# Decode attention plus bilinear GLU on one core: the query weights of head 0 leave the first load and come with the second

## The chip, the cores and the metric

The kernel runs on one core of a Trainium2 chip. The metric is the device time of one execution in microseconds (us). The kernel before the change takes 377.63 us, the median of three runs (377.3 to 377.72). One more execution was taken with the hardware profiler: it took 377.5 us, and the trace of it spans 375.7 us; some 1.8 us of the time lie around the span.

## The reference

One token is decoded for a batch of two, in float32. `x` has 2 rows of 512 values. It is normalised to `xn` (mean and variance over the 512), and three things are added:

```python
xn = _layernorm(x, axis=-1)
return x + _A_ref(xn, A_k_cache, A_v_cache, A_wq, A_wo) + _B_ref(xn, B_w_gate, B_w_up, B_w_down)
# A: q = xn @ wq (32 heads of 128); scores = q . K / sqrt(128); p = softmax(scores); o = p . V; o @ wo
#    K and V: the last 2048 positions of each head's cache, for each of the two batch rows
# B: ((xn @ w_gate) * (xn @ w_up)) @ w_down, inner width 1376
```

Nearly all data are the caches: 2 x 32 x 2048 x 128 values for K and as many for V, each used once.

## The kernel before, in words

**The stream.** All inputs but a small copy of `x` are laid out on the host in one DRAM array, `stream`, in the order in which they are used. `blocks()` (L43 to L79) lists the loads: each is a list of fields (kind, index, width in floats for each of the 128 partitions). Each load is one DMA of 128 rows, one row to a partition. The first load goes to a tile of its own, `first`, that stays; the others go to three rotating buffers, `step`, of 13,824 floats a partition (`BUFS = 3`). `pump()` (L141) issues loads on SP's queue, in order, until all three buffers are taken. `done()` (L164) counts the fields of a buffer; when the last field is used the buffer is free, and `pump()` issues the next load into it.

In the kernel before, the loads begin so (rows in floats for each partition; 4 bytes each):

| load | fields | floats in a row | KB in all |
|---|---|---|---|
| first | x (8), columns of ones: pick, rows, carry (31), w of head 0 (512) | 551 | 275.5 |
| step 0 | w of heads 1 to 3 (1536), K and wq of heads 0 and 1 | 10752 | 5376 |
| step 1 | half of w_gate and w_up, K and wq of head 2 | 12800 | 6400 |
| step 2 | the other half, K3, V0, K4 and their weights, parts of w_down | 13440 | 6720 |
| step 3 on | three K or V units each | 13824 | 6912 |

Here `wq` beside K of head h is a quarter of the query weights of the group of four heads after h's own. The query weights of heads 0 to 3 alone are needed at once; they are the fields `w 0` (head 0) and `w 1` (heads 1 to 3).

**The start.** DVE (VectorE) and PE (TensorE) make the layer norm from `x` (L211 to L229) and spread `xn` over 128 columns each (`xnb`), so that a matmul with it puts q into all 128 partitions. `project_first(0)` then multiplies `xnb` with `w 0` into a part of the PSUM tile `tr` (8 matmuls of 128 columns, which the trace shows as 16 passes), and `project_first(1)` multiplies it with `w 1` into the PSUM tile `q` (8 matmuls of 384 columns, 16 passes). Both stand in the code in this order, in a loop ahead of the heads, and each engine runs its instructions in the order of the code (the class `InOrder`).

**A head.** For head h: `products(h)` on DVE multiplies K by q in place (4096 elements a partition), `project_q(h)` on PE makes a part of a later group's q, `sums(h)` on DVE adds over the 128 elements and frees K, `maxima(h)` finds the largest score, `weights(h)` makes the exponentials on ACT (ScalarE); POOL (GpSimd) reduces over partitions. `products(0)` reads q from `tr`; `products(1)` to `products(3)` read it from the tile of `project_first(1)`. Three heads later `values` multiplies with V on PE and adds the output projection into `acc`. `project_gu` and `gate` (heads 2 and 3) do the GLU between. The last loads are small pieces, so that little is left to do when the last one lands.

In the trace almost every instruction has line L97, that of the helper in `InOrder`, so groups are told apart by engine, tile and shape.

Of the kernel before, what the change touches and what calls it, by code (L numbers as in the profile page):

```python
# [17 lines left out]
B, D, H, DH, SK, F = 2, 512, 32, 128, 8192, 1376  # L18
W = min(4096, max(256, SK // 4))
J = W // P  # L20
NC = D // P
# [12 lines left out]
CK, CQ, CO = B * J * DH, NC * GC, D  # L34
# [9 lines left out]
def blocks():  # L44

    def wd(n):
        return [("wd", i, D) for i in range(*WD[n])]

    def k(h):
        return [("k", h, CK)] + ([("wq", h, CP)] if h + HG < H else [])

    def v(h):
        return [("v", h, CK), ("wo", h, CO)]  # L60

    def gu(half):
        n = NC * (FH[half][1] - FH[half][0])
        return [("wg", half, n), ("wu", half, n)]

    units = []
    for h in range(LAG, H - 1):
        units += [k(h), v(h - LAG)]
    ones = [("pick", 0, 8 * B), ("rows", 0, NFB * B), ("carry", 0, M)]
    first = [("x", 0, B * NC)] + ones + [("w", 0, NC * DH)]  # L70
    loads = [[("w", 1, CQ - NC * DH)] + k(0) + k(1), gu(0) + k(2)]
    loads += [gu(1) + units[0] + units[1] + wd(0) + [("wr", 0, NS * P)]]
    loads += [sum(units[i : i + 3], []) for i in range(2, len(units), 3)]
    loads += [k(H - 1) + v(H - 1 - LAG) + wd(1)]
    out = [(("f", 0), first)] + [(("s", i), fields) for i, fields in enumerate(loads)]
    late, last = ("s", len(loads)), ("s", len(loads) + 1)
    out += [(late, v(H - 3)), (late, v(H - 2)), (last, [("v0", H - 1, CL)])]
    out += [(last, [("v1", H - 1, CK - CL)]), (last, [("wo", H - 1, CO)] + wd(2))]
    return out + [(last, wd(n)) for n in range(3, len(WD))]  # L79
# [33 lines left out]
def kernel(  # L113
# [19 lines left out]
    for key, fields in blocks():  # L133
        todo.append((key, fields, at))
        at += P * sum(w for _, _, w in fields)
# [312 lines left out]
    for _, fields in blocks():  # L448
        ks = [i for kind, i, _ in fields if kind == "k"]
        vs = [i for kind, i, _ in fields if kind == "v"]  # L450
        if vs and vs[-1] >= H - 5:
            break
        for n, h in enumerate(ks):
            products(h)
            project_q(h)
            if 2 <= h <= 3:
                project_gu(h - 2)
            sums(h)
            if h == LAG:
                gate()  # L460
            if vs and n == 0:
                values(vs)
            if h == LAG:
                down(0)
                down_rest()
            maxima(h)
            weights(h)
            if h >= 1:
                reciprocals(h - 1)
# [52 lines left out]
def laid_out(x):  # L522
# [3 lines left out]
    a = x["A_x"].reshape(B, D)  # L526
    first = {
        kind: np.zeros((P, w), a.dtype) for kind, _, w in blocks()[0][1][:4]
    }
    first["x"][:] = a.reshape(B, P, NC).transpose(1, 0, 2).reshape(P, B * NC)  # L530
# [83 lines left out]
```

## Time and profile before

| | |
|---|---|
| time, median of 3 runs | 377.63 us (377.3 to 377.72) |
| profiled execution | 377.5 us, its span 375.7 us |
| PE busy | 254.2 us in 1084 matmul passes |
| DVE busy | 294.1 us in 146 instructions |
| ACT busy | 58.6 us |
| POOL busy | 25.3 us |
| bytes moved by DMA | 159.70 MB, 425 GB/s over the span |

Times in the trace are microseconds from the start of the span. A row of the timeline has start, duration, engine, line, operation, the tile written and the tiles read, the shape, the count, and in brackets how long the engine had been idle before and what ended it. A row of the table by stretch has, for each engine, the busy time in the stretch and the number of instructions, then the granted clock of PE (1.00 is full), the share of the time in which the 16 DMA engines were busy (short stretches can show more than 1, since a packet is put down to where it starts) and the rate. A line of DMA issues has the size of one and the time from its issue to its landing.

### The profile page before, as it was taken

The numbers are of one execution on the slowest core, as the hardware profiler recorded it, in microseconds if no ns is written. First come the engines' busy times: TensorE is split into PE (matmuls) and PEld (weight loads), VectorE is DVE, ScalarE is ACT, GpSimd is POOL, SyncE is SP. The second block draws the span as 40 slices with busy tenths as digits, with TensorE's granted clock in tenths as the row PEclk, the third lists the DMA queues.
The fourth block names the chain that finished last, engine by engine and source line by source line (L and its number), as shares of the span: only waits on it lengthen the run. The fifth ranks groups of instructions, "written<-read, shape, count | busy, mean of one in ns | idle before, by whom it ended". The sixth has DMA issues, their size and how long they took to land.

```text
span 375.7 us, 2858 instructions
## 1 busy us (share of the span) xinstructions
PE 254.2 (68%) x1084; PEld 88.5 (24%) x1084; DVE 294.1 (78%) x146; ACT 58.6 (16%) x259; POOL 25.3 (7%) x78
## 2 busy tenths in 40 slices
PE   3496497886547486854858476685846669637996
PEld 3241023331112122211212121231212122212334
DVE  3299691998599499769949976994996799599950
ACT  1021001122021111201112020211202011211131
POOL 1001000000000000100000100000000000000010
PEclk9998967998697666888768696885869676857999
DMA  8999999899999999999999999999999999999995
GB/s 346 445 436 454 426 408 471 383 465 449 395 466 406 442 455 400 459 418 436 460 400 449 424 430 459 402 442 430 430 459 406 437 444 436 419 431 443 398 421 221
DMA packets 4492, 159.70 MB, mean 425 GB/s; under 512 B 512, under 2 KB 640, under 8 KB 1152
## 3 DMA queue, kind: packets, MB, share of 16 engines
q1 hardware_dynamic: 4480, 159.54, 98.5%
q8 instruction: 8, 0.13, 0.1%
q14 instruction: 4, 0.03, 0.0%
HBM read 159.48 MB, written 0.06 MB: 425 GB/s over the span
## 4 chain that ended last, share of the span: by engine, by line
DMA 63%; DVE 26%; PE 8%; ACT 1%; issue 0%; SPq 0%; DVEq 0%
DMA step<-in_stream_dram 63%; DVE s L97 13%; DVE step L97 13%; PE o_ps L97 3%; PE q L97 2%; PE acc L97 2%; PE tr L97 1%; ACT o_sb L97 0%; DVE m L97 0%; ACT oT L97 0%; SPq L97 0%; DVE rec L97 0%; DVE o_out L97 0%; DVEq L97 0%
## 5 line engine op out<-in xcount | busy, mean ns | idle before, releaser
L97 DVE TENSOR_TENSOR step<-step,q 128x4096 f32<-128x4096 f32 x31 | 136.6, 4407 | 52.4 <-DMA step<-in_stream_dram 52.4
L97 PE MATMUL q<-step,xnb 128*128 128x512 f32 (+1 forms) x128 | 92.4, 872 | 76.4 <-DMA step<-in_stream_dram 76.4
L97 DVE TENSOR_REDUCE s<-step 128x32 f32<-128x4096 f32 x32 | 141.4, 4419 | 1.1
L97 PE MATMUL o_ps<-step,p 128*16 128x512 f32 x512 | 68.9, 672 | 11.5 <-DMA step<-in_stream_dram 11.5
L97 PEld LDWEIGHTS q<-step,xnb 128*128 128x128 f32 x128 | 32.3, 275 | 130.5 <-DMA step<-in_stream_dram 77.5
L97 PE MATMUL acc<-step,oT 128*9 128x512 f32 (+1 forms) x88 | 35.4, 552 | 9.3 <-ACT oT L97 8.1
L97 PE MATMUL tr<-first,o_sb 128*128 128x2 f32 (+2 forms) x198 | 28.1, 261 | 15.4 <-ACT o_sb L97 13.0
L97 ACT COPY o_sb<-o_ps 128x512 f32<-128x512 f32 (+1 forms) x25 | 14.1, 568 | 140.7 <-PE o_ps L97 140.7
L97 PEld LDWEIGHTS tr<-first,o_sb 128*128 128x128 f32 x198 | 26.0, 200 | 36.8 <-ACT o_sb L97 32.4
L290 POOL PARTITION_ALL_REDUCE mm<-m x32 | 11.3, 354 | 283.1 <-DVE rec L97 180.1
L97 PEld LDWEIGHTS o_ps<-step,p 128*16 128x16 f32 x512 | 13.4, 104 | 69.9 <-issue 54.4
L97 ACT ACTIVATE nm<-mm 128x2 f32<-128x2 f32 x32 | 6.5, 203 | 131.4 <-POOL mm L290 131.4
L97 ACT ACTIVATE p<-s,nm 128x16 f32<-128x16 f32 x64 | 19.2, 300 | 1.0
L97 ACT ACTIVATE oT<-tr,rec 128x1 f32<-128x1 f32 x64 | 12.2, 260 | 28.5 <-PE tr L97 28.5
L306 POOL PARTITION_ALL_REDUCE sum<-rs x32 | 12.7, 398 | 55.0 <-ACT p L97 55.0
L97 PE MATMUL o_ps<-step,xn 128*2 128x512 f32 (+1 forms) x48 | 13.9, 616 | 0.0
L97 ACT ACTIVATION_READ_ACCUMULATOR p<-s,nm 128x1 f32 x64 | 12.0, 187 | 0.0
L97 DVE TENSOR_TENSOR step<-step,tr 128x4096 f32<-128x4096 f32 x1 | 4.4, 4422 | 9.3 <-DMA step<-in_stream_dram 9.3
L97 PEld LDWEIGHTS acc<-step,oT 128*9 128x9 f32 x88 | 4.5, 91 | 19.4 <-ACT oT L97 12.7
L97 PE MATMUL q<-xnb,mean_w 128*128 128x512 f32 (+2 forms) x18 | 8.3, 551 | 0.0
L97 DVE TENSOR_TENSOR o_out<-acc,x_nat 128x128 f32<-128x128 f32 x1 | 0.3, 292 | 8.8 <-PE acc L97 8.8
L97 DVE TENSOR_REDUCE m<-s 128x2 f32<-128x32 f32 x32 | 5.9, 186 | 1.1
(39 smaller groups left out, 40.5 us busy)
## 6 DMA issues: line engine op xcount, KB each, us to landing
step<-in_stream_dram SPq DMA_DIRECT2D x16, 6912.0 KB, 31.1
step<-in_stream_dram SPq DMA_DIRECT2D x2, 6400.0 KB, 32.8
step<-in_stream_dram SPq DMA_DIRECT2D x1, 6720.0 KB, 45.4
step<-in_stream_dram SPq DMA_DIRECT2D x1, 6656.0 KB, 29.0
step<-in_stream_dram SPq DMA_DIRECT2D x1, 5376.0 KB, 15.3
step<-in_stream_dram SPq DMA_DIRECT2D x1, 4864.0 KB, 29.6
step<-in_stream_dram SPq DMA_DIRECT2D x2, 2304.0 KB, 17.1
step<-in_stream_dram SPq DMA_DIRECT2D x1, 1536.0 KB, 14.6
```

The source lines that it names most:

```text
L97: made = call(*args, **kwargs)
L290: nc.gpsimd.partition_all_reduce(mm, m, P, bass_isa.ReduceOp.max)
L306: nc.gpsimd.partition_all_reduce(sum_t[h], rs, P, bass_isa.ReduceOp.add)
```

## The change

The first load keeps only `x` and the columns of ones: 39 floats, 156 bytes a row. `w 0` moves to the front of step 0, whose rows grow from 10752 to 11264 floats. Nothing else is changed: `project_first(0)` finds its weights in the step buffer, and its `done("w", 0)` now counts towards freeing that buffer. The order of the instructions on every engine is as before, and so is the number of DMAs.

```diff
     ones = [("pick", 0, 8 * B), ("rows", 0, NFB * B), ("carry", 0, M)]
-    first = [("x", 0, B * NC)] + ones + [("w", 0, NC * DH)]
-    loads = [[("w", 1, CQ - NC * DH)] + k(0) + k(1), gu(0) + k(2)]
+    first = [("x", 0, B * NC)] + ones
+    w = [("w", 0, NC * DH), ("w", 1, CQ - NC * DH)]
+    loads = [w + k(0) + k(1), gu(0) + k(2)]
     loads += [gu(1) + units[0] + units[1] + wd(0) + [("wr", 0, NS * P)]]
```

## The prediction

> **What bounds the kernel now.** I read the page first, then a table by stretch, then the timeline of the first 70 us and of the end.
>
> ```profile
> PE 254.2 (68%) x1084; PEld 88.5 (24%) x1084; DVE 294.1 (78%) x146; ACT 58.6 (16%) x259; POOL 25.3 (7%) x78
> ...
> DMA  8999999899999999999999999999999999999995
> ...
> q1 hardware_dynamic: 4480, 159.54, 98.5%
> q8 instruction: 8, 0.13, 0.1%
> ...
> DMA 63%; DVE 26%; PE 8%; ACT 1%; issue 0%; SPq 0%; DVEq 0%
> ```
>
> DVE is busy for 78% of the span and PE for 68%, but the 16 DMA engines for 98.5%: their line is 8 or 9 in every slice until the last. The chain of waits puts 63% on the arrival of `step` loads. Its 26% on DVE are no bound of their own: that chain goes from a load's issue back to the DVE work that freed the buffer, and whether the issue was late has to be looked at by itself. The table by stretch shows that it was not (columns: the five engines' busy time, PE's granted clock, share of DMA, GB/s):
>
> ```profile
> 3.50:16.40 12.90, 4.93 (x20) 4.49 (x20) 1.83 (x9) 0.26 (x1) 0.00 (x0) 1.00 1.01 437
> 16.40:47.40 31.00, 22.44 (x60) 8.02 (x60) 27.03 (x11) 3.97 (x16) 2.26 (x6) 0.93 1.01 436
> 47.40:65.10 17.70, 15.23 (x46) 5.79 (x50) 9.70 (x5) 1.71 (x8) 0.35 (x1) 0.69 0.96 413
> 65.10:81.40 16.30, 13.70 (x64) 4.88 (x56) 16.05 (x6) 3.56 (x16) 1.15 (x3) 0.94 1.00 434
> 81.40:340.70 259.30, 166.80 (x650) 52.50 (x648) 216.08 (x97) 39.86 (x184) 18.06 (x48) 0.76 1.00 433
> ```
>
> From 3.5 us to 340.7 us the share is 1.00 or 1.01 and the rate 433 to 437 GB/s in every stretch but one: in 47.4 to 65.1 us a load takes 17.7 us where the next takes 16.3. So the loads flow one behind the other with no hole, and each load's place in time is the sum of the bytes ahead of it. The end hangs on them too:
>
> ```profile
> 372.49 0.12 PEld L97 LDWEIGHTS acc<-step,hT 128*9 128x9 f32 x8 [0.30 <-DMA step<-in_stream_dram]
> 372.96 0.29 DVE L97 TENSOR_TENSOR o_out<-acc,x_nat 128x128 f32<-128x128 f32 x1 [8.80 <-PE acc L97]
> ```
>
> The weight load of PE's last group waited 0.30 us for the last load's landing; 0.47 us later DVE makes the last addition. The time is therefore: when the stream begins, plus 159.5 MB at its rate, plus a tail of some 3.2 us from 372.49 to 375.7.
>
> **The change part by part: the stream.** No byte is added. 512 floats a row (256 KB over 128 rows) go from the first load to the second. Both are in front of everything else, so all later loads start after the same bytes, 551 + 10752 = 39 + 11264 floats a row. What can differ is the start.
>
> SP's rows of the timeline to 40 us, one line on the packets that began by 1.73 us, and the issues to 2.8 us (size, time to landing):
>
> ```profile
> 0.72 0.38 SPq L97 DMA_DIRECT2D first<-in_stream_dram  x1
> 1.16 1.37 SPq L97 DMA_DIRECT2D step<-in_stream_dram  x3
> 2.57 0.54 SPq L97 DMA_DIRECT2D x_nat<-in_x_rows_dram  x1
> 34.54 0.33 SPq L97 DMA_DIRECT2D step<-in_stream_dram  x1
> ```
>
> ```profile
> DMA packets 2, 0.00 MB, mean 3 GB/s; under 512 B 0, under 2 KB 0, under 8 KB 2
> ```
>
> ```profile
> step<-in_stream_dram SPq DMA_DIRECT2D x1, 6720.0 KB, 45.4
> step<-in_stream_dram SPq DMA_DIRECT2D x1, 6400.0 KB, 30.0
> step<-in_stream_dram SPq DMA_DIRECT2D x1, 5376.0 KB, 15.3
> first<-in_stream_dram SPq DMA_DIRECT2D x1, 275.5 KB, 2.9
> ```
>
> SP issues the first load at 0.72 and the next three from 1.16 in a row of 1.37 us, some 0.46 each. Two packets had begun by 1.73, so data starts to flow 1.0 us after its issue. First (275.5 KB) takes 2.9 us to landing; the load after it (5376 KB) lands 15.3 us after its issue, thus at 16.5. Now the first transfer shrinks to 19.5 KB. What its eight rows for each engine cost is bounded by a transfer of rows of a like size, the output at the end (56 KB in rows of 512 bytes; its stretch is 373.0 to 375.7):
>
> ```profile
> q1 hardware_dynamic: 128, 0.06, 7.6%
> ```
>
> 7.6% of 2.7 us are 0.205 us an engine for 8 packets, 26 ns each. For 156 bytes I take at most that, 0.2 us. The 256 KB that move cost 0.60 us at 437 GB/s, in the first load or in the second. So two ends. If the second load's data flow as soon as the small rows are through, the stream keeps its place, or gains at most some 0.1 us, the price of eight separate packets an engine. If the second load cannot flow sooner than it does now (its issue at 1.16 is not moved; today the share of DMA is full from 3.5 on, as the first load lands), the 0.60 us are in full a hole: +0.6 us. By the issue, 0.44 us after the first one and with the same 1.0 us to first data, it can flow from 2.2 us, about when the small rows end. That is near the lower end: I take **+0.1 us**. Nothing hides it: this cost is on the path in full.
>
> [...]
>
> **The change part by part: q of head 0 comes late.** PE's and DVE's rows of the timeline:
>
> ```profile
> 7.20 3.75 PE L97 MATMUL tr<-first,xnb 128*128 128x128 f32 x16 [1.53 <-issue]
> 16.52 11.84 PE L97 MATMUL q<-step,xnb 128*128 128x384 f32 x24 [5.57 <-DMA step<-in_stream_dram]
> 31.62 2.65 PE L97 MATMUL q<-step,xnb 128*128 128x512 f32 x4 [3.26 <-DMA step<-in_stream_dram]
> 34.20 8.02 PE L97 MATMUL o_ps<-step,xn 128*2 128x512 f32 x32
> ```
>
> ```profile
> 16.58 4.42 DVE L97 TENSOR_TENSOR step<-step,tr 128x4096 f32<-128x4096 f32 x1 [9.33 <-DMA step<-in_stream_dram]
> ...
> 25.59 4.41 DVE L97 TENSOR_TENSOR step<-step,q 128x4096 f32<-128x4096 f32 x1
> ...
> 47.48 4.42 DVE L97 TENSOR_TENSOR step<-step,q 128x4096 f32<-128x4096 f32 x1 [3.67 <-DMA step<-in_stream_dram]
> ...
> 65.25 4.42 DVE L97 TENSOR_TENSOR step<-step,q 128x4096 f32<-128x4096 f32 x1 [7.16 <-DMA step<-in_stream_dram]
> ```
>
> The 16 passes into `tr` ran from 7.20 to 10.95, while the second load was under way; DVE then waited 9.33 us for that load alone. Now they too wait for it. PE starts at 16.52 as before, but with these 16 passes: 3.75 us, from 16.5 to 20.3. The row is taken as it is: those passes followed an idle PE (1.53 us, and small passes before), and so will these, after a longer one. `products(0)` follows the last pass instead of the landing (PE's 16.52 and DVE's 16.58 stand side by side today), so **DVE starts 3.75 us later**, at 20.3. The moved wait holds up, on PE, the 16 passes of heads 1 to 3 and `project_q`; on DVE, the two memsets are ahead of it and everything else behind.
>
> PE's groups by shape to 31 us:
>
> ```profile
> L97 PE MATMUL q<-step,xnb 128*128 128x384 f32 x16 | 8.4, 703 | 5.6 <-DMA step<-in_stream_dram 5.6
> L97 PE MATMUL tr<-first,xnb 128*128 128x128 f32 x16 | 3.8, 429 | 1.5 <-issue 1.5
> L97 PE MATMUL q<-step,xnb 128*128 128x512 f32 x8 | 3.6, 592 | 0.0
> ```
>
> On PE, the 16 passes of heads 1 to 3 (8.4 us) then end at 28.7 instead of 24.9. `products(1)` wants them when DVE is there: 25.59 + 3.75 = 29.3, so 0.6 us to spare. They cannot take longer than in the trace, where they followed 5.6 us of idle PE; even 1 us more would only add itself to DVE's delay. Behind them the 8 passes of `project_q` (3.6 us) end at 32.3, 0.7 us after the 31.62 at which PE now waits for the next load; `project_gu` (34.20, 8.02 us) then ends at 42.9 at the latest, before DVE has done head 2.
>
> Who waits for DVE? First, SP: the fourth `step` load is issued at 34.54, when head 1's sums free the first buffer. It becomes 38.3. Its data are wanted when the third load is through; that landed 45.4 us after its issue at about 2.1, thus at 47.5. With 1.0 us from issue to data it has to be issued by 46.5: 12 us to spare today, **8.2 us** after the change. The fifth issue moves by as much, and has the 17.7 us that the fourth load flows as well. Second, DVE itself: after head 2 it waited 3.67 us for the load with K3, until 47.48. The delay of 3.75 us eats that wait and leaves 0.1 us, which the next waits (7.16 us before 65.25) take. So after head 3 DVE is where it was. If this cover were not there, the price would be the whole 3.75 us; it is there twice, in the loads already issued and in DVE's own waits.
>
> **What is won** is nothing on the path: `x` lands sooner than now (0.72 + 2.9 = 3.6), but the norm's chain ends ahead of the passes at 7.20, and the next load is not there before 16.5.
>
> **Sum.** +0.1 us for the start, 0 for the rest. The profiled execution's 377.5 us would become 377.6; it lies 0.13 us below the median, which becomes **377.7**.
>
> **The rivals.** *A full hole at the start.* The second load begins when it begins now. For it: today the first load's data cover its start, so the trace doesn't show how early it could. Against: its issue is early enough by 0.44 + 1.0 us. Price +0.6, 378.2 us, still within 0.2%.
>
> *The lag of one DMA engine, on the slow side.* A load has landed when the slowest of 16 engines has done its rows. The load of 47.4 to 65.1 took 17.7 us instead of 16.3, and in it lies this:
>
> ```profile
> q8 instruction: 1, 0.02, 5.8%
> ```
>
> That is a fetch of instructions on a queue of its own in the 1.0 us from 51 to 52: 5.8% of 16 engines, 0.93 us of one engine. The lag of 1.4 us then stays to the end; the other fetches (8 in all, the page's q8 line) add nothing to the landings, so I take it that they fall on engines that were not last. The change moves PE's first passes and the engines' places in the first 16 us, and so may put a second fetch on the engine that is already behind. It decides from the second fetch on the same engine: +1.4 us, with the +0.1 **379.1 us**, slower. Against it: that from 65.1 to 340.7 no load lags again, through several fetches, looks like turns taken, not chance; and the three runs lie within 0.42 us.
>
> [...]
>
> *The stream gains.* The same lag on the other side: if the start leaves the fetched engine ahead of the others by as much as the fetch takes, the 1.4 us are saved: 376.2 to 376.9 us. For it: only the spread of the engines after the start decides it. Against: first and second load land with all engines within a fraction of a us, for else the stretches would not each show a share of 1.0.
>
> *A new wait in place of the old.* That q of head 0 stalls the stream would need an issue to be wanted more than 9 us ahead of its data; then each us of it costs one, up to 3.75. The first load's 1.0 us speaks against it; I put it with the slow cases. That the change doesn't do what it says is excluded by the loads' lengths.
>
> **How the numbers follow.** The forecast (a start within +-0.3 us) 0.52, at 377.4 to 378.0; the full hole 0.15, at 378.2; the slow cases (second fetch on one engine, a longer hole, a late issue) 0.22, at 378.4 to 379.1 and above; the gain 0.11. 0.2% is 0.75 us, about what a measurement of this kernel can tell from no change: 376.9 and 378.4 are its bounds. So faster 0.11, same 0.67, slower 0.22. The range 377.0 to 378.9 leaves out about 0.1 on each side.
>
> **What would show it.** In the changed kernel: the first landing before 3.2 us; 16 passes into `tr` from about 16.6, and DVE's first multiplication at about 20.4, released by PE; the fourth issue at about 38.3; DVE's wait before head 3 near zero, that before 65.3 still about 7 us; the landing for head 4 at 65.2 to 65.5; shares of 1.00 in all stretches to 340 us. Wrong it would be if the second load landed later than 17.1, if a stretch after 47 us had a share under 0.98 beyond the one lag, or if the stretch of 17.7 us came twice or not at all.

## The result and the profile after

| | before | after |
|---|---|---|
| time, median of 18 runs each, in turns on one chip | 377.43 us (377.26 to 377.85) | 378.17 us (377.99 to 378.57) |
| profiled execution | 377.5 us, span 375.7 us | 378.18 us, span 376.4 us |
| end of the second load, mean of the 16 DMA engines (from the packets' records) | 15.85 us | 16.46 us |
| the same, slowest engine | 16.15 us | 17.36 us |

After stands to before as 1.0019, with a 95% interval of 1.0012 to 1.0026: 0.74 us or 0.196% slower. The forecast was 377.7 us with a range of 377.0 to 378.9. The time lies in the range, and the loss is just inside the 0.2% that the prediction took as no change; but it is there, and it has the size of the first rival, the full hole at the start (378.2).

From the page of after, the share of the DMA engines and the chain of waits:

```profile
q1 hardware_dynamic: 4480, 159.54, 98.3%
...
DMA 55%; DVE 24%; PE 18%; ACT 1%; issue 1%; SPq 0%; DVEq 0%
```

The bytes and the number of packets are those of before, and DMA still bounds the kernel. The table of after by stretch, cut at the landings:

```profile
3.50:17.70 14.20, 0.59 (x3) 0.50 (x2) 1.67 (x8) 0.26 (x1) 0.00 (x0) 1.00 0.96 413
17.70:48.70 31.00, 21.45 (x76) 10.15 (x76) 26.89 (x11) 3.07 (x11) 1.50 (x4) 0.95 1.01 436
48.70:65.40 16.70, 14.24 (x50) 5.03 (x50) 9.63 (x7) 2.61 (x13) 1.11 (x3) 0.81 0.98 425
65.40:81.70 16.30, 13.72 (x60) 5.17 (x56) 16.10 (x6) 3.56 (x16) 1.15 (x3) 0.92 1.00 434
81.70:341.40 259.70, 170.10 (x650) 52.85 (x648) 216.05 (x97) 39.86 (x184) 18.06 (x48) 0.76 1.00 434
```

Here the first stretch stands out: 0.96 and 413 GB/s to 17.7 us, where before it was 1.01 and 437 to 16.4. From 17.7 us on the stream is as full as it was. The issues of step 2, of step 0 and of the first load of after (size, issue to landing) say the same:

```profile
step<-in_stream_dram SPq DMA_DIRECT2D x1, 6720.0 KB, 46.6
...
step<-in_stream_dram SPq DMA_DIRECT2D x1, 5632.0 KB, 16.5
...
first<-in_stream_dram SPq DMA_DIRECT2D x1, 19.5 KB, 1.8
```

`x` lands at 0.72 + 1.8 = 2.5 us, 1.1 us sooner; step 0 lands 16.5 us after its issue, at 17.7, 1.2 us later. Both landings, 16.5 us in before and 17.7 in after, lie 0.3 us behind the end of the slowest of the 16 engines (16.15 and 17.36); in the mean of the engines step 0 ends 0.61 us later. The rest is one engine, whose second row of step 0 (from 4.71 us) took 2.68 us instead of 1.67. No fetch of instructions stands beside that row, and its cause is open. PE and then DVE in the timeline of after:

```profile
17.81 3.75 PE L98 MATMUL tr<-step,xnb 128*128 128x128 f32 x16 [13.06 <-DMA step<-in_stream_dram]
21.35 8.96 PE L98 MATMUL q<-step,xnb 128*128 128x384 f32 x24
```

```profile
21.60 4.42 DVE L98 TENSOR_TENSOR step<-step,tr 128x4096 f32<-128x4096 f32 x1 [15.27 <-PE tr L98]
...
39.56 9.38 SPq L98 DMA_DIRECT2D step<-in_stream_dram  x2
...
48.75 4.40 DVE L98 TENSOR_TENSOR step<-step,q 128x4096 f32<-128x4096 f32 x1
...
65.50 4.42 DVE L98 TENSOR_TENSOR step<-step,q 128x4096 f32<-128x4096 f32 x1 [7.13 <-DMA step<-in_stream_dram]
```

The 16 passes take 3.75 us behind the landing, and DVE's first multiplication starts 5.02 us later than before (16.58): 3.75 for the passes and 1.2 for the landing. Its wait before head 3 is gone (no bracket at 48.75); before head 4 it waits as long as ever, and there it is only 0.25 us behind.

**Where the loss arises.** The first 2.7 us of both streams in 40 slices of 0.0675 us, first after, then before:

```profile
DMA  0000000000000000000000000454211199999000
```

```profile
DMA  0000000000000000000000000935999935577799
```

Data begin in slice 26, at about 1.7 us, in both. In after the small rows leave holes until the long rows start, the first at 2.2 us (the zeros at the end are not idle: a packet is put down to where it starts). By the packets' records an engine is through with the small rows at 1.97 us in the mean and starts its first long row at 2.36 (2.20 to 2.87), so it stands idle for 0.40 us. In before an engine goes from the last row of the first load to the first long row, at 2.94 in the mean, without a gap.

The first long row on each engine is slow as well. The queue's row for after's stretch of 2.2 to 2.9 us and for 7.8 to 9.0 us:

```profile
q1 hardware_dynamic: 15, 0.63, 298.3%
```

```profile
q1 hardware_dynamic: 15, 0.68, 130.1%
```

The first has 14 long rows and a packet of a few bytes: 298.3% of 16 engines for 0.7 us are 33.4 us, 2.39 us a row. The second has 15 rows in 25.0 us: 1.67 us a row. Each engine has 8 rows of step 0 and pays **0.72 us too much on the first of them**. In before, by the packets' records, the 16 first rows (2.75 to 3.3 us) last 1.78 us and the later ones 1.59, 0.20 too much. But before pays in its first load too. Of its 2204-byte rows, 94 begin by 2.7 us:

```profile
q1 hardware_dynamic: 94, 0.21, 33.1%
```

These are 14.3 us of engine time, 152 ns a row, where the last ones take 89 ns. The account for a mean engine, from the packets' records (in brackets what the rows took over the pace of the later ones of their size):

| | before | after |
|---|---|---|
| its 8 rows of the first load | 1.08 us (0.37) | 0.14 us (0.03) |
| idle until its first long row | 0.01 us | 0.40 us |
| its 8 rows of step 0 | 12.93 us (0.22) | 14.12 us (0.80) |

The 256 KB cost 0.60 us in either load. What is left of the 0.61 us between the two is idle time (0.39 more) and slow long rows (0.58 more), less the slow rows of before's first load (0.34 less); the remaining 0.02 us are in when the first rows start.

### The profile page after: what moved, and what is told of

Same layout as the page of the kernel before. It is cut to its first block, busy times and chain, and to the rows that moved or that the text cites. A ratio compares the mean times of both kernels' runs of the same rounds, so it can differ in the third digit from the quotient of the medians.

```text
span 376.4 us, 2859 instructions
## 1 busy us (share of the span) xinstructions
PE 252.5 (67%) x1084; PEld 87.1 (23%) x1084; DVE 293.8 (78%) x146; ACT 58.6 (16%) x259; POOL 25.3 (7%) x78
## 3 DMA queue, kind: packets, MB, share of 16 engines
q1 hardware_dynamic: 4480, 159.54, 98.3%
## 4 chain that ended last, share of the span: by engine, by line
DMA 55%; DVE 24%; PE 18%; ACT 1%; issue 1%; SPq 0%; DVEq 0%
DMA step<-in_stream_dram 55%; DVE s L98 12%; DVE step L98 12%; PE o_ps L98 7%; PE q L98 4%; PE acc L98 4%; PE tr L98 4%; ACT o_sb L98 1%; ACT oT L98 0%; DVE m L98 0%; ACT hT L98 0%; DVE o_sb L98 0%; SPq L98 0%; DVE rec L98 0%; ACT hX L98 0%
## 5 line engine op out<-in xcount | busy, mean ns | idle before, releaser
L98 PE MATMUL o_ps<-step,p 128*16 128x512 f32 x512 | 71.1, 692 | 12.1 <-DMA step<-in_stream_dram 12.1
L98 PE MATMUL tr<-first,o_sb 128*128 128x2 f32 (+2 forms) x198 | 26.6, 253 | 15.5 <-ACT o_sb L98 13.0
L98 PEld LDWEIGHTS tr<-first,o_sb 128*128 128x128 f32 x198 | 24.6, 191 | 37.3 <-ACT o_sb L98 32.7
L98 PE MATMUL tr<-step,xnb 128*128 128x128 f32 x16 | 3.8, 429 | 13.1 <-DMA step<-in_stream_dram 13.1
L98 PE MATMUL o_ps<-step,xn 128*2 128x512 f32 (+1 forms) x48 | 11.9, 548 | 0.0
## 6 DMA issues: line engine op xcount, KB each, us to landing
step<-in_stream_dram SPq DMA_DIRECT2D x1, 5632.0 KB, 16.5
step<-in_stream_dram SPq DMA_DIRECT2D x2, 2304.0 KB, 17.1
```

What stands on the lines that cost most here:

```text
L98: made = call(*args, **kwargs)
```

## The experiments

**Theories.** *Slow start*: at the start an engine stands idle or moves rows slowly; the 2204-byte rows of the first load used to fill that phase (the cover), and now the long rows of step 0 meet it. *Small rows*: rows of 156 bytes are costly by themselves. *Late q*: the 3.75 us on DVE cost something after all. Each run is set against runs of before on the same chip (377.39 to 377.46 us); ratios have 95% intervals.

**e1: q stays late, the first load has its old size.** After, with wq of head 0 (512 floats, not urgent) in the first load:

```diff
-    first = [("x", 0, B * NC)] + ones
+    first = [("x", 0, B * NC)] + ones + k(0)[1:]
     w = [("w", 0, NC * DH), ("w", 1, CQ - NC * DH)]
-    loads = [w + k(0) + k(1), gu(0) + k(2)]
+    loads = [w + k(0)[:1] + k(1), gu(0) + k(2)]
```

> The first load is as long as before (551 floats a row) but holds the 512 floats of wq of head 0 that head 5 of the stream's queries need later, while w of head 0 comes in the second load as in the change. If the cover of the second load's start is the cause, the time is that of the kernel before, 377.4 us (377.2 to 377.7), although DVE starts some 3.75 us late. If the late q is the cause, it is that of the changed kernel, 378.2.

377.34 us against 377.39, 0.9999 (0.999 to 1.0008). DVE's rows in e1's timeline:

```profile
20.46 4.42 DVE L98 TENSOR_TENSOR step<-step,tr 128x4096 f32<-128x4096 f32 x1 [13.25 <-PE tr L98]
...
47.61 4.40 DVE L98 TENSOR_TENSOR step<-step,q 128x4096 f32<-128x4096 f32 x1
...
65.11 4.42 DVE L98 TENSOR_TENSOR step<-step,q 128x4096 f32<-128x4096 f32 x1 [7.89 <-DMA step<-in_stream_dram]
```

q is as late as the prediction had it (20.46), and the whole loss is gone. The loss hangs on how much the first load holds.

**e2: before's loads, q held back.** A matmul of two columns of `w 1` makes the first passes wait for step 0:

```diff
+    pe.matmul(
+        tr[:, 3 * P : 3 * P + 2], mean_w, got["w", 1][0][:, 0:2], start=True, stop=True
+    )
     for i in range(2):
         project_first(i)
```

> The loads of the kernel before, untouched; one extra matmul of two columns that reads the second load stands ahead of the projection of head 0, so that q of head 0 is as late as in the changed kernel. If the start of the stream is the cause: 377.4 us, the same as before. If the late q is the cause: 378.2 or a little more.

377.50 us against 377.39, 1.0002 (0.9994 to 1.0011), with DVE's first multiplication at 20.96. The late q alone costs nothing that can be measured; this theory is out.

**e3 and e4: after with zeros behind the ones.** 512 floats of padding in e3 (rows of 2204 bytes, 256 KB more in all), 89 in e4 (`P - 39`: rows of 512 bytes, 44.5 KB more). The edit of e3, without the line that makes the zeros:

```diff
-    first = [("x", 0, B * NC)] + ones
+    first = [("x", 0, B * NC)] + ones + [("pad", 0, NC * DH)]
```

> The changed kernel with 512 floats of zeros a row added to the first load, which nothing reads: 256 KB more in all, 0.60 us at 437 GB/s. If the change only opened a hole of about that size at the start, the added bytes are free: 378.0 to 378.2 us, like the changed kernel. If the hole is not the cause, they are paid on top: 378.8.

377.99 us, 1.0014 (1.0005 to 1.0023). The first long rows take 0.17 us too much instead of 0.72, and 256 KB more cost 0.60 us at the stream's 437 GB/s. Padding the first load to its old size is paid for by what it saves: after is not slower with more to move.

> The changed kernel with 89 floats of zeros a row added to the first load, which makes its rows 512 bytes long: 44.5 KB more. If rows below 512 bytes are the cause, it is back near the kernel before, 377.5 us. If the shortness of the whole first load is the cause, it stays near the changed kernel: 378.0 to 378.3.

378.95 us, 1.0042 (1.0029 to 1.0056). Neither theory had this: rows of 512 bytes should have been as good as after or better. The first long row was slow as in after (2.43 us), so the larger rows had mended nothing, and something more was lost. The records show where: the 55,296-byte rows of the later loads take longer, 2046.9 ns in the mean against 2043.3 in after. The first tile grew by 352 bytes, and with it the step buffers moved in SBUF, the on-chip memory, from byte 28,416 of a partition to 28,768.

**e7 and e8: only the place in SBUF.** e7 is e4 with 160 bytes left free ahead of the buffers (they then begin at 28,928); e8 is before with 32 bytes left free (30,496 instead of 30,464). The edit of e8 (in e7, 40 floats on top of e4):

```diff
     const = ctx.enter_context(tc.tile_pool(name="const", bufs=1))
+    gap = const.tile([P, 8], F32, name="gap")
+    nc.gpsimd.memset(gap, 0.0)
```

> The run with rows of 512 bytes again, with 160 bytes left free ahead of it in each partition, so that the step buffers begin at a multiple of 64 bytes again as they do in the kernel before; the addresses in DRAM are those of the run with 512 bytes. In that run every long row took 3 to 5 ns more to the end of the stream. If the place in SBUF is the cause, the rows take 2041 ns again and the time is that of the changed kernel, 378.1 to 378.3 us; if the place in DRAM is, it stays at 378.95.

> The kernel before with 32 bytes left free in each partition ahead of everything, so that the step buffers begin at 32 bytes past a multiple of 64; DRAM as before. If the place in SBUF is the cause of the slower rows: 378.1 to 378.2 us, rows of 55,296 bytes at 2044 ns. If the place in DRAM is: 377.4 and 2041 ns.

e7: 378.35 us, 1.0021 (1.0013 to 1.003). e8: 378.75 us, 1.0032 (1.0019 to 1.0044). The long rows last 2043.2 ns in e7, and 2049.6 in e8 against 2044.2 in before. DVE's waits for the loads in e8, of which the first and last were 65.25 and 325.17 in before:

```profile
65.56 4.42 DVE L97 TENSOR_TENSOR step<-step,q 128x4096 f32<-128x4096 f32 x1 [7.02 <-DMA step<-in_stream_dram]
...
326.37 4.42 DVE L97 TENSOR_TENSOR step<-step,q 128x4096 f32<-128x4096 f32 x1 [4.26 <-DMA step<-in_stream_dram]
```

e8 falls from 0.31 to 1.20 us behind along the stream, with no other change than the 32 bytes (and the instruction that clears them). So what e4 loses beyond e7 (1.56 us against 0.91, each to before on its own chip) was the place of its buffers. e8 lost more than was expected of it, 378.75 us where 378.1 to 378.2 stood: besides the slower rows, its load near 79.6 us begins with slow rows (0.21 us in the mean), of which more below. e7 is where after is, with 44.5 KB more (0.1 us): rows of 512 bytes are no better than rows of 156.

**e9: after with 384 floats in front.** `wr` (part of w_down, used late) goes from step 2 into the first load: rows of 1692 bytes.

```diff
-    first = [("x", 0, B * NC)] + ones
+    wr = [("wr", 0, NS * P)]
+    first = [("x", 0, B * NC)] + ones + wr
...
-    loads += [gu(1) + units[0] + units[1] + wd(0) + [("wr", 0, NS * P)]]
+    loads += [gu(1) + units[0] + units[1] + wd(0)]
```

> The change, but with other 384 floats a row (a part of w_down that comes with the fourth load otherwise) moved into the first load: 423 floats ahead of the second load instead of 39 or 551, no byte added. If what counts is how long the first load's data last, the loss of 0.74 us shrinks by about 384 / 512 of it: 377.5 to 377.7 us. If the loss has nothing to do with the amount ahead: 378.2.

377.73 us against 377.46, 1.0007 (0.9998 to 1.0015). Its first long rows take 0.40 us too much, between before and after, and so is its time.

**e5 and e12: more cover than before.** e5 puts wq of heads 0 and 1 behind `w 0` in before's first load (rows of 6300 bytes); e12 puts `wr` there (3740 bytes).

```diff
-    first = [("x", 0, B * NC)] + ones + [("w", 0, NC * DH)]
-    loads = [[("w", 1, CQ - NC * DH)] + k(0) + k(1), gu(0) + k(2)]
+    first = [("x", 0, B * NC)] + ones + [("w", 0, NC * DH)] + k(0)[1:] + k(1)[1:]
+    loads = [[("w", 1, CQ - NC * DH)] + k(0)[:1] + k(1)[:1], gu(0) + k(2)]
```

```diff
-    first = [("x", 0, B * NC)] + ones + [("w", 0, NC * DH)]
+    first = [("x", 0, B * NC)] + ones + [("w", 0, NC * DH), ("wr", 0, NS * P)]
...
-    loads += [gu(1) + units[0] + units[1] + wd(0) + [("wr", 0, NS * P)]]
+    loads += [gu(1) + units[0] + units[1] + wd(0)]
```

> The kernel before with more in the first load: wq of heads 0 and 1 (1024 floats) move there from the second load, so the first has rows of 6300 bytes. If the second load's slow first rows are covered by whatever flows ahead of them, the rest of 0.2 us that the kernel before still pays (first rows of 1.6 to 2.3 us where 1.59 is the steady time) is covered too: 377.1 to 377.3 us. If the cover is already complete: 377.4, the same as before. The norm starts some 1.2 us later, which is not on the path by the late-q run.

> The kernel before with 384 floats more in the first load (the same part of w_down): 935 floats ahead of the second load. If the cover was complete with 551 floats: 377.4 us, no gain. If some of the start is still open, 377.2. The run with 1575 floats gave 377.9 at the same mean landing of the second load, so a loss of some 0.1 to 0.2 us is possible too.

e5: 377.90 us against 377.44, 1.0012 (1.0003 to 1.0021), a miss. e12: 377.39 against 377.46, 0.9999 (0.999 to 1.0007). The first long row takes 0.07 and 0.10 us too much, less than the 0.20 of before, but nothing is won that can be measured. In e5 the engines end the second load at 15.84 us in the mean, as in before, but the slowest at 16.47 instead of 16.15. Why rows of 6300 bytes spread the engines stays open.

**e6: w 0 as a load of its own.** x and the ones first, `w 0` in a second DMA, then before's step 0:

```diff
-    first = [("x", 0, B * NC)] + ones + [("w", 0, NC * DH)]
+    first = [("x", 0, B * NC)] + ones
...
-    out = [(("f", 0), first)] + [(("s", i), fields) for i, fields in enumerate(loads)]
+    out = [(("f", 0), first), (("f", 1), [("w", 0, NC * DH)])] + [(("s", i), fields) for i, fields in enumerate(loads)]
...
-                    tiles[key] = const.tile([P, n], F32, name="first")
+                    tiles[key] = const.tile([P, n], F32, name=f"first{key[1]}")
```

> The first load as in the change (39 floats a row), then w of head 0 as a load of its own (2048 bytes a row), then the second load of the kernel before. If only the start of the long rows has to be covered, the 0.6 us of w of head 0 cover it, and what is left of the loss is the gap after the small load and one more issue of 0.46 us: 377.5 to 377.8 us. If any short first load costs the whole: 378.2.

378.04 us against 377.44, 1.0016 (1.0007 to 1.0025), a miss. SP's rows of e6:

```profile
0.72 0.85 SPq L97 DMA_DIRECT2D first<-in_stream_dram  x2
1.62 1.37 SPq L97 DMA_DIRECT2D step<-in_stream_dram  x3
```

Here q is early again, and step 0's rows are nearly cured (0.27 us too much), yet the time is almost after's. The rows of the `w 0` load are hardly slow (0.06 us an engine in all), but up to the first long row an engine stands idle for some 0.7 us: between the small rows and those of `w 0`, which begin at 2.2 us, and between these. So slow rows alone do not make the loss; idle engines cost as much. Step 0 is also issued 0.46 us later.

**e10 and e11: the second load issued sooner.** If a late issue were the cause, step 0 should gain by an issue at 0.72. The first load goes to ACT's queue, and step 0 becomes the first in SP's; e10 is after, e11 is before with this edit.

```diff
-            sp.dma_start(tiles[key][:, c0:c1], src)
+            (act if key[0] == "f" else sp).dma_start(tiles[key][:, c0:c1], src)
```

> The changed kernel with its first load issued by ACT instead of SP, so that SP issues the second load at 0.72 us instead of 1.16. If the loss is the time in which the small load is through and the second does not flow yet, it is gone: 377.3 to 377.6 us, even if x lands later beside the long rows. If long rows at the head of the stream cost it whenever they come: 378.1 to 378.3.

> The kernel before with the same edit: the first load on ACT, the second on SP at 0.72 us. By the cover theory the kernel before has little left to gain: 377.2 to 377.5 us. If the two queues disturb each other: above 377.7.

379.12 us, 1.0045 (1.0033 to 1.0057), and 380.09, 1.0059 (1.0041 to 1.0077). e10 is far off both of its forecasts; e11 is on the side of queues that disturb each other. From e10's issues, its queue between 1.7 and 3.2 us, and its timeline:

```profile
first<-in_stream_dram ACTq DMA_DIRECT2D x1, 19.5 KB, 16.4
```

```profile
q1 hardware_dynamic: 16, 0.72, 158.6%
```

```profile
24.52 4.42 DVE L98 TENSOR_TENSOR step<-step,tr 128x4096 f32<-128x4096 f32 x1 [3.74 <-PE tr L98]
...
78.61 0.33 SPq L98 DMA_DIRECT2D step<-in_stream_dram  x1
```

The 16 first rows take 158.6% of 16 engines for 1.5 us, 2.38 us each: long rows that start at once are as slow as after's. So an earlier issue does not cure the slow rows. But it closes the idle time: the mean end of step 0 is 16.05 us against 16.46 in after and 15.85 in before, so some two thirds of the 0.61 us are won back. Against that stands a new cost. Of the 19.5 KB on the second queue no row begins between 1.7 and 3.2 us (the 16 packets of that stretch are long rows), and they land 16.4 us after their issue, about when step 0 does (16.3 after its own); x is late, DVE starts at 24.52, 7.9 us behind before, and the cover of the prediction is used up: the issue that stood at 72.90 in before comes at 78.61. The stretches of 72 to 78 and 78 to 84 us of e10:

```profile
72.00:78.00 6.00, 5.41 (x13) 1.13 (x13) 5.97 (x4) 1.20 (x7) 0.75 (x2) 0.72 1.00 433
78.00:84.00 6.00, 5.29 (x34) 2.25 (x31) 5.33 (x3) 0.59 (x1) 0.00 (x0) 1.00 0.84 323
```

323 GB/s instead of 433: there the stream has run dry for a moment (0.22 us an engine in the mean, by the packets' records), and the first rows of the load that was issued at 78.61 are slow, of which more below. No run beat before by more than its interval.

The cover in one table (bytes of the first load's rows; eight rows an engine lie ahead of step 0's; the third and fourth columns are means of the engines from the packets' records):

| kernel | row of the first load | idle ahead of the first long row | from the issue of step 0 to its first row | first long row over the steady one | time over before |
|---|---|---|---|---|---|
| after | 156 B | 0.40 us | 1.2 us | 0.72 us | 0.74 us |
| e7 | 512 B | 0.44 us | 1.4 us | 0.73 us | 0.91 us (44.5 KB more) |
| e9 | 1692 B | 0.05 us | 1.6 us | 0.40 us | 0.27 us |
| before | 2204 B | 0.01 us | 1.8 us | 0.20 us | 0 |
| e1 | 2204 B | 0.01 us | 1.9 us | 0.17 us | -0.05 us |
| e12 | 3740 B | 0.01 us | 2.2 us | 0.10 us | -0.07 us |
| e5 | 6300 B | 0.01 us | 3.1 us | 0.07 us | 0.46 us |

**Slow rows are those of a load that was issued shortly before.** The fifth column falls as the fourth grows, and this is not peculiar to the start of a kernel. The load that begins near 79.6 us was issued late in four runs, and there its first rows are slow too, after 78 us of stream: 0.57 us too long in e10 (issued 1.4 us before the first rows, in the mean), 0.22 in e11 (3.1 us), 0.11 in e5 (3.1 us) and 0.21 in e8 (3.3 us). In every trace the first rows of a load of long rows that was issued 5 us or more ahead are at the steady pace, to 0.04 us. The runs were not built to vary this time alone, so it is an observation and not an experiment; but it speaks against the engines' own warming up.

## Why the prediction was right, and where not

**DMA bounds the kernel, no byte is added.** Held: 159.54 MB in both, and after the start shares of 1.00 and above but for the 0.98 of one lag.

**The small rows.** 128 rows of 156 bytes were put at no more than 26 ns each. After's queue from 1.7 to 2.2 us:

```profile
q1 hardware_dynamic: 145, 0.11, 88.1%
```

These are 7.05 us of engine time; without the two long rows in it (4.7 us) some 16 ns a packet, about 0.13 us for eight. The bound held. Rows of 512 bytes gained no time: e7, which has them, took 378.35 us, after 378.17. The rows of 156 bytes do move less for their time (11 bytes a ns, against 19 for e7's 512-byte rows and 27 for the long ones), but on 19.5 KB that is under 0.1 us, by an estimate from these figures.

**The start, +0.1 us: this step failed.** The prediction reasoned that the second load's data can flow from 2.2 us by its issue, "about when the small rows end", and so took the lower end of -0.1 to +0.6. The first long rows do start at 2.2, but two things were put at nothing. The small rows end sooner than that: by the prediction's own figures at 1.73 + 0.2 = 1.93 us, and in the trace at 1.97 in the mean, with the long rows from 2.36. That is 0.40 us of idle engines, which before fills with rows of `w 0`. And the first long row was priced at its steady duration; it lasts 0.72 us too long, 0.52 more than before's. Against both stands only that before's first load had slow rows too (0.37 us). The mean end of the second load moves from 15.85 to 16.46, by 0.61. That is the upper end of the bounds, and the price of the rival "full hole", though the load begins 0.58 us sooner than in before (2.36 against 2.94) and not, as that rival had it, when it begins now. The criterion set beforehand, a landing of the second load later than 17.1, was met: it came at 17.7. That the time lies in the range is owed to the width of the range, not to this step. Before's own rows of 2.75 to 3.3 us had the sign: 1.78 us for rows that later take 1.59.

**q of head 0 comes late, at no cost: right.** The 3.75 us were those of the trace. The 16 passes of heads 1 to 3 behind them, put at 8.4 us at most, took 5.5 (499 ns each, against 703 in before, where they followed 5.6 us of idle PE). The fourth issue came at 39.56 instead of 38.3, with 7 us still to spare, because the landing was late; DVE's waits took it. e1 and e2 show this with 20.46 and 20.96. That the cover is finite is shown by e10, where 7.9 us were too many.

**The lag of one engine.** It neither doubled nor went away, but moved. In before the fetch at 51.13 us holds an engine for 0.93 us, and the row behind it takes 2.55 us instead of 2.04; together they are the 1.4 us, of which the prediction had seen the 0.93. In after one engine is late since 4.71 us, the fetch comes at 57.50, and the stretch of 17.7 us became 16.7. DVE's waits later in the stream, in before and in after:

```profile
163.02 4.42 DVE L97 TENSOR_TENSOR step<-step,q 128x4096 f32<-128x4096 f32 x1 [5.31 <-DMA step<-in_stream_dram]
195.68 4.42 DVE L97 TENSOR_TENSOR step<-step,q 128x4096 f32<-128x4096 f32 x1 [5.37 <-DMA step<-in_stream_dram]
...
325.17 4.42 DVE L97 TENSOR_TENSOR step<-step,q 128x4096 f32<-128x4096 f32 x1 [4.12 <-DMA step<-in_stream_dram]
```

```profile
163.39 4.42 DVE L98 TENSOR_TENSOR step<-step,q 128x4096 f32<-128x4096 f32 x1 [5.45 <-DMA step<-in_stream_dram]
196.70 4.42 DVE L98 TENSOR_TENSOR step<-step,q 128x4096 f32<-128x4096 f32 x1 [6.01 <-DMA step<-in_stream_dram]
...
325.86 4.42 DVE L98 TENSOR_TENSOR step<-step,q 128x4096 f32<-128x4096 f32 x1 [4.22 <-DMA step<-in_stream_dram]
```

After is behind by 0.37, then 1.02, at the end 0.69 us. The landings follow the slowest engine (0.3 us behind its end at step 0), so these differences swing with the engine that a fetch of instructions has hit: after has one at 190.67 us, 0.95 us long, and by the packets' records its engine ends that load at 196.17 us, the others by 195.56. The mean of the engines is 0.61 us behind at step 0 and some 0.47 from 243 us on; the slowest engine, which ends the stream, is 0.69 behind at the last input load. e1 shows that the whole 0.74 us hangs on what the first load holds; how much of it is the mean and how much the one late engine is not told apart.

**What stays open.** Why the first rows of a load issued shortly before are slow. It does not take all 16 engines beginning at once: behind a fetch, a single engine's next 55,296-byte row takes 0.47 to 0.54 us longer in before, while the other 15 keep their pace, though that load was issued long ago. Whether that is the same delay, no run shows.

## What to carry to other kernels

In a kernel that a DMA stream bounds, what goes first has to be enough to keep the engines busy until the rows of the next load can flow at their pace: here some 2 KB a row, eight rows an engine, that are needed anyway. Shrinking the first load to get the first operands sooner bought 1.1 us for a chain that had slack, and lost 0.7 us for the one that had none. When a step says "it can start at t", ask when the rows ahead of it end, and read the first row's duration beside its start.

## What the runs showed of the hardware

- **A load issued shortly before its first rows.** Its first long rows are slow: 0.72 us too long 1.2 us after the issue, 0.20 after 1.8 us and 0.07 after 3.1 us, all at the start; near 79.6 us, 0.57 after 1.4 us and 0.11 to 0.22 after 3.1 to 3.3 us. After 5 us or more it is no more than 0.04 us in any trace.
- **The place of a buffer in SBUF.** Rows of 55,296 bytes took 2049.6 ns in e8 against 2044.2 in before, with the buffers moved by 32 bytes; the median row took 2045 against 2041, which over 128 such rows an engine is 0.5 us. e4 and e7 differ in the place alone, and in what they lose to before by 0.65 us. The faster rows went to buffers that began at byte 30,464 (before), 28,416 (after) and 28,928 (e7), the slower ones to 30,496 (e8) and 28,768 (e4): the first three are multiples of 64, and also of 256, the other two lie 32 bytes past a multiple of 64. The runs agree in sign and show 3 to 4 ns in the median. They do not tell 256 from 64, and why the place counts they do not show.
- **The fetch of instructions.** One fetch held one engine for 0.93 us, the row behind it took 0.5 us longer, and a landing lay 1.4 us late (the stretch of 17.7 us in before): by the packets' records that engine ended the load at 64.78 us, the next one at 63.45.
- **A small load on a queue of its own.** Beside the long rows of another queue, 19.5 KB took 16.4 us to land in e10 and 275.5 KB as long in e11; in front of them, on their queue, these took 1.8 us in after and 2.9 in before.
